# Taking the three lowest weight bits with a ScalarE Copy instead of a VectorE shift, in a fused scan and FFN kernel

## The chip, the core and the metric

The kernel runs on one core of a Trainium2 chip. The metric is the device time of one execution in microseconds, the median of several runs. The engines are TensorE (PE: matmuls, PEld: weight loads), VectorE (DVE), ScalarE (ACT), GpSimd (POOL) and SyncE (SP), whose queue issues nearly all transfers.

## What is computed

A gated linear attention with a complex decay runs over 768 steps for 4 batches and 8 heads of 48 columns; its output is the input of a feed-forward part with a rational activation. The reference, cut to what matters:

```python
for t in range(S):                          # S = 768, D = 48
    S_re, S_im = ar*S_re - ai*S_im + kv, ar*S_im + ai*S_re
    y[:, :, t] = einsum('bhd,bhde->bhe', q[:, :, t], S_re)
x = y.transpose(0, 2, 1, 3).reshape(B*S, H*D)   # 3072 x 384
h = x @ w_in                                     # 384 x 2048
g = (a0 + a1*h + a2*h**2 + a3*h**3) / (1 + |b0|*|h| + |b1|*h**2 + 1e-6)
out = g @ w_out                                  # 2048 x 384
```

`w_in` and `w_out` are 64-bit floats. The kernel gets them as 64-bit words and has to make 32-bit floats of them.

## The kernel before, in words

The sequence is cut into 6 chunks of 128 steps; with 4 batches that makes 24 units, taken in pairs. For a unit `norm` (lines 459 to 487) makes magnitudes and running products, `angle` the phases, `trig` their sines, `outer` the turned q and k, which go through DRAM into the layout HQ, and `attn` (lines 564 to 626) the scores, values and state, and ends in xT, the transposed input of the FFN. `ffn` (from line 629) takes a pair: eight steps k of two 128-row slices of the hidden layer each. The matmuls into ph (line 642) need xT and the weight tiles wi; five ScalarE and four VectorE operations make g out of ph; the matmuls into po (line 659) need g and wo. The first two pairs use the 32-bit weights as they are; then `split` halves each weight into two parts for faster matmuls.

`fold` (lines 407 to 418) makes one 32-bit weight tile of a tile of 64-bit words, 28 times: 12 tiles wi of 128x512 and 16 tiles wo of 128x384. A transfer brings the words into a staging buffer (rings g with four buffers, and wh0, wh1, wh2). An Abs on ScalarE with scale 2^-112 takes the upper word, read as a float, into the tile; a multiplication by zero on VectorE or GpSimd leaves the sign alone in the upper word; a VectorE operation shifts the tile left by 3 and ors the sign in; a second one shifts the lower word right by 29 and ors its three top bits in. Then the staging buffer is free for the next transfer of its ring. These two are in the trace as SCALAR_TENSOR_TENSOR on uint32, with wi or wo as the output.

Nothing is scheduled at run time: every operation is a Plan.op with the engines that it may run on and a cost for each. `recorded` (line 175) reads the order of all 2733 operations, with the engine of each, out of the string ORDER, and they are issued in that order, so each engine and the SP queue run their own part of it in sequence. If an operation waits, all that follows on its engine waits too. ORDER was found by a search over the plan's costs (`list_schedule`).

Of the kernel before, what the change touches and what calls it, by code (L numbers as in the profile page):

```python
# [222 lines left out]


ORDER = (
    "c-lpndwkC2|Ht2-F?L|rHN<As=6o*SPEJLUMF`oxLQRg}oSMj?atb*`q?xlAeJh78Q4ygMDXAf8jyY{cKG$L!#r^(0@B915@8Q8cpZoe;*Zc5#zh19vBH>a|"
    "lH?!#M~zIBdAdhi$v*8UuSr|=q=FRlO)UQgfAS<+Zs{GZDTR7i+UP~CBd0V`3N%bs$|U_=D@p?2#Y%)+(6Z84{?yBQOUp^7Ow-NMTo=h4J;xj8Oon?oQj4wJ"
    "&;>G1OY|OzmBrFkD@i4JUKVLUf7aC!$#;`wnU0XMQdbVEnkjy)jArLNov%Y|Q#Vr2=u|u1UoVepYw0Xicw>$%;QgcezPzDLWPsc&XW9Rf7HcCptrK(tdAv!?"
    "lUY})cgq>=9QAGZ%kGv=;k3D0P5Mfr?DgUU6=az??9UYPG!<NZEs`Gki44^$vPIhIE@{Ayec7dw?d!JaOL9=BYjv3<L&)?a?IUrly;}xJRq3U3r4#SGBl-G<"
    "J|sR-WSUCu3CYsurHL6Y<6OQb$ZdT^zarjVx`IsZlU%JV$zea<sUTCR_*8jZhHFyTkAZ?fr?6djZtCMyVxp|qfm9`$%HIl|pW`jM6Cstndn1pRgh^>2!8;YG"  # L230
    "?3Dy!rMBeBI(<$WnOqkxw|P3=jCGM9psd`Ci7ukV=Bk@vX1Vej<~gmYm*hg=E-zNj2i}&cQeMhwSudUMZ)uFAnu=mwkybZjizX(HIaAMjPM7OHU?E9f(CXe*"
    "9k16llirr-C>^J>WC0Pz%9)tTZmblURqS%Fbkr=#XLlcr_!^}z*$KY&?qZjb(og4^?(TpLHS^s9A}vF0=S!MdqOnE8^>uv<)C}YEM>zu4K9+rfObO@=T}Yj)"
    "%TnpA8S<eX)@JepwI8Do*%U{nbb7XorJk`;XeVErDdUN9jUHsp3XP_ZSrX}`1?I^uDNEd*ZRmQjZ)M&bqtl3Xv23JEs;_~V|C*D2yj<3Lbh^4s)MAtGPm<|c"
    "Uw+q>-V1?-GK7;W$wh4_{lIsBKFflb2_Sr|x#~{?11B{_zZNTlIbp3C;nLZAwLR~z)zjKdv!#sGk`o#ZazE3)62{z316{4837_S~*g<|RdB9}5H`$}5>FHF*"
    "OOYN3WXm9Lpw^QA1n&1%Yd=|SzIQpM&`*>!%>~z4>{(6@$Y9pwnA?75Spo{X66+x?0K297gACAI?IGJuZ?{}iIqgIKXZhxD{me9Rb-{l+{T(V_>o|!sPrJ97"
    "!do#5+$jBzyhDW(v<q1u&~186p3!gUYF~K-7T8F|W5~C^UFw&GYi7tu%{2{OroG$$O&U_q2jy?gGSQOa0vg4+&%y|6wJuYUl+^m{2%;ayB)`w3y<k7{-__TN"
    "<$3vDi@;2=R+X#ztuB{Rv(f*aIvoX#k@RA&US*y?_vdSxybUAW(Cxa?X8HSdfV{4QWRs>4)jrMBAxvFsGI|gkUbIvFoqE~~bgd-b?(*NFzinZhzFNgz@vo7;"
    "m6v6<egO}Tk)|+Sp}eHQC;y^?LnT8;%RBlLOmLFf{}BE;BX<H7y!~d0AIW*1bhFz+Kcz_vJJb)Cmh}96ovnFNUw6wL6X!PTO`WPonBZ1&*_`ux%0~DogG^Ux"
    "dHAIlC@j&*a7{J(n<m|1?H9oESLOp)Y^<*3X&G4$hU(jR_c~o@DGPO(T+vOS{u`L~PrU?lCM7jJTdG%dv<BDiw6px}+JT9#Y&*KHGE7#pW}I#Sk#)&=nXU)X"
    "@7eZ#7dp63&cTnWd(A_x3Y@i8`kL7;MSj*)vRDK&+$Hnv3coy9?Cq+_yV^^ln9gSMoq5U?YG0G-g84L(CPcqkztlBSQ&yPHZk2u`OLZ+BiUNHrwT|gn^t6t)"  # L240
    "E#R+IaIx78ay`r%=TXDuD8P2}g?krXs}0^RlV7s^#Lqy#Qs~ZAeHZK$nsxpdSUFh?Q7xgem%(ytU25977o`tcR-K=Q%Qh6zH?>`fK4Me-A)v4VXGF0gSL4hT"
    "rtJWAeMDZR=FRNipsgI(?E=3vWb%iiI!{S=JxAT{ljlIjO?}a>_k-AY(SGDVBd5XZ3=l9J{JpIg=xT|MrB=g1XE|wX+q(?*iqX^XMO%q-J%~R5+Go@CFF@^C"
    "-KBNxQU3>RV-Ndd*=L^qk$CJ(S9s#ln4zwjSBENO=mmX3lI0WTs4DZAr(NY^Eo(X#MaqBmRid0m9~;R+xtramF?)Hsk<Wg1j=u*apW(DHSszoUC|ldf(~=dF"
    "TC|ajOW}uWX0_X(Tl7gZw<%iP9%c7ns2r2$52H%o!CG15lmp_PwcGuHF!W|Kn10uWqnp}st|j{Zj`_+TZ|k@n<~}eGMpS)p7r!JfK08di!!hsaWg<?;4?Gk4"
    "Zl@kM#-+ji*TKaSyTcFYTpecL^Sj9wB5Th#vsmp>rPHjh!ycYIB)^g89$lnC4qwc)9Ki?7;<FBsHstRlnWc@XM+VQj(ysw>hz>{NiY}RZLCiwdoYCJj)mC>4"
    "^bK|$kDdhGL;$DM!0vJDnWI_oWHue&54QhiexfB_`k6<Vpr7?T8ax=}Jt?o-Hq63NqC8Jco(Z(}c54r_&$eU&zo1_W;oO?MQOM-f$5~~=)YtJkll9*`|Ac)8"
    "$>+K#P}5rvn?5CvNjm%z%sSY!(|Qp8`irb56G@6(F~@bMzl^Fz$?cdvMV(l)RWt1SelC5RO#I_;RhvvpmxaH{G|^0Gj%n`tODeHMlW7(Dy@yE~uTP_Pdttj7"
    "?54US$Y5aPS8XdhKu$ofpa$={5uk21Pflo>UFX-uooo-e$u%%wn)J4t{Rk@e3R<SRKjc1hn6~y*ye0i@gX(tEZFURHn9j2XvRv<y1}O9(dyl_KeqolH@joAS"
    "U7>%W_S1<YfHqYk&S;q+C(Qf2+t?oT%W&Sup(&eS+Q~8h6`d(}h-CzPG6z;z4I^ZN_seijcXB<9gZPrFY+y|Xuv~~{og%tBaKsgS%U0aiBB~10NPB%o-q!QD"
    "=ES7>XZPq<sR4=(>#0Ds*o#`uS7}Y&yKG0llwBSKX^Y^5pG~Z*!P%2=MRP!t^IO6z<vDu?-e{HH#3A;w9sI|c*I()TEc|Q=KQ#sihfE_EAwiGc$#wzvN6lOp"  # L250
    "&x$nW=A?eFgUNplUUHkxH7~hBQw{bircc%2xmW2^w0xHse)b8eM<ng(N<6AntV?v8tTX%lKGMo2`$Kt>OxzXu%%XBbq#aIaCJLKFz7=7-aK713ub(2yEpnU="
    "l<NHwBM-=oP?wWIZmG7AhwV(ivUJjH8|4~H1-r+erJF!~a9*yV%2CoqqHU&&gs+2)*8x}54;4GDpTUB=O_)QyLk!SKK4s!=Fuf^sW2<^zN2Vczn)IYH3ph7V"
    "*VqdFc<OM1JIYb*Zfm>$Rn^xBCVqon(<!o>t}P?8{&?Au=y4&jjKYcBB${lny_FkC3iEXbe|=Jq2gFNde&@17RolTW!b=6H!VMI?FPKl2@sdJKTf^na*K)nX"
    "8pkc=3VV&xi8?m6wVz547lW{T-Dg_3FzGKZnp9j$hSs&M+*a-cGw}SSFy$%TZCCpvm~0ORS%wbvX2KSkU+^5q(D(xFZ$82coCXo!(6>Xp_b4c>4tl$zW4D-)"
    "Qhn0y#o^55ydg|UD)W(Viu{*Q=<Y;19UXcc?R|{*YRLVlK{~E0hm}|8NH$nHq$f>ZDfUmHMGEeI#b4K8-za&`X3)KPbfXze_okKuIWe$TB|5eeROg0fY&N;S"
    "Awf0YVWQY=I^16aZ&i#6WNL~%=I=tKZnF1I{n`#ky9_G6QES@-_b0t*Aw8Ik0=#=7dVN#(qB*0b1N)!C@eRP;W>K-qpb(w+AEHVN><m0$Q)YEGo}#{tg5lb^"
    "`u1KoLEh3srix1l>2^)}@C|Fv={lzUcw&;P;ws7p+y{3~@O2gDIv03TJ^<BU`YE{CgwR}F*GYPv`$s*d_hFf$mO7;Ia}G@QlU}g7{vo{A1NK?B5f?ibh3YBY"
    "^iytvAL$Ox&0!KsaW6TzlS}fN-sbcfx(a8x)c*_o{RL*G+5~@~6qtB74kUf<dz_ue`Ylogb*LyE;lMN64L-fDNnSIY>teXG12ftIcT<_3yh7ahC_xF6G%zXh"
    ">_V9n_zL}-0r&5un;uvRhd~!eGT5q5FJ6;3ZCgLw9)O#YbuYK}fi~aYO{aS^e_7m}hY&-Ml^c-tYNq-CT|7#M+Jq|2?bW>u`xVPn=JN)cb^sUt0e!w?EN<)s"
    "D^J37k=*;My6L)#%GBdV@GAOy8I^2KR-fw+tRE%M()luQ)&y8#uFS{%Hpf>t#l7^TR^@T~*ZGW)(e!U77|aDV*O-K4v_jF?c)D~*>oEJ1c-E1=e1MKTU`M(W"  # L260
    "Xv+fnGZn7MhUKoCRsJM%9;J>3y#?g)DM+u%RNSNGy_wn>b}(pkuxq1W%+a!0gS)pO)}R+!$@Hn>!_dfh-min+rrS;aa-9QTTp-`7(g7Zuz&p2?g^H|xj`_Hx"
    "50Lc$`6qGhnPNJ5ILIM^MqX9<PWtE(ZbvJ)G3+Jk4cxy<$l_yNhRZ(;5B^AeKD_iKHOXV`lX$9F@_9-o%46_uTu85~$x3dJ!O03^kCxQ#G?TZP>Xhmy<_-66"
    "x)vduOo}_Dzvv6pZyaa7XWF7g=^*6<`Zj`mf_JTN?Lts>jrGACkDzvI^hNGw<Cutld1LS(7qyp7_nUD;&15#?h$cZ=+cMl0bG1K;a0+#6rNiKxE!1~UAl%E8"
    "NAbiFyrI<gK`=PSjCQ-Zcg9o0S>|guQft~*9k(r_n5g?;;bK!0N74iA6=+3U%l$-cinTXq-VHjlV7ssUu3(@<12NAQ?VvJCwF10<8Kl;hX7U$G5lw6!&SIwq"
    "eM||RJg5)bIJb+Rdx772tgD3*Tq2TA?7r1>aeL^_K>Bq<5Ar-fwLEarRW5KFxW(<HCu|!5B5K(rSBYKYLN|?{VUdfffnUgND|e)NK?UI!{JS1QwOg?6CVkp#"
    "lHmWV+@a^0J}#)1AEBzz@I^XaBLY9t#a4B}F8+wqC_&SYF{_14{svTOFtJ|Jg><B?l$cuXk_K-iJ7DUXA?K68+*J$ha~h1+b8+xVbm)|9;!hyXOYGQ(S!|Av"
    "3s$BE+Sr8ECA@tC2lz**62Whh<PVs3KNY%2y({CFmCpv~o5ut;m;YDSBPjJfOy4=GU(H=nHHq##Yol0`YudZ(+!Uf<f@`qKpS*pRTeJsC8n7aUn4&@o6AcId"
    "st+?WH#jqoCwp*t`E<UTi{{iDeA^tQ+lnVW2}X8vlPu8SZz=O(caJ^tna)zZZkoD+&>X}ug(Xa38LCo|eWOs3>L~IlZq=7VU8@!P4d?%U(|HH}EiiYvf9QB5"
    "-aSHsH3^s78vN@?S$tzz&I$f0hYtvF##{J=F#ePYJ^eqdrFae"
# [691 lines left out]
```

## Time and profile before

| | |
|---|---|
| median of 3 runs | 622.45 us (619.75 to 622.86) |
| profiled execution | 623.88 us, span 622.17 us |
| mean granted TensorE clock | 0.979 |
| busy share of PE, DVE, ACT, POOL | 88%, 89%, 82%, 49% |
| moved by DMA | 64.87 MB |

How to read it: a busy share is an average over stages. The table of stretches gives busy microseconds of each engine in a stretch of the span; the list of waits tells which engine ended an idle time; the timeline gives single instructions with their start, their duration and, in brackets, the idle time before them and what ended it. A duration includes some overlap with the next instruction of the engine, so the pitch of two neighbours is the better price.

### The profile page before, as it was taken

The numbers are of one execution on the slowest core, as the hardware profiler recorded it, in microseconds if no ns is written. First come the engines' busy times: TensorE is split into PE (matmuls) and PEld (weight loads), VectorE is DVE, ScalarE is ACT, GpSimd is POOL, SyncE is SP. The second block draws the span as 40 slices with busy tenths as digits, with TensorE's granted clock in tenths as the row PEclk, the third lists the DMA queues.
The fourth block names the chain that finished last, engine by engine and source line by source line (L and its number), as shares of the span: only waits on it lengthen the run. The fifth ranks groups of instructions, "written<-read, shape, count | busy, mean of one in ns | idle before, by whom it ended". The sixth has DMA issues, their size and how long they took to land.

```text
...
## 1 busy us (share of the span) xinstructions
PE 546.5 (88%) x6786; PEld 502.1 (81%) x6786; DVE 556.0 (89%) x986; ACT 511.8 (82%) x880; POOL 304.1 (49%) x255
## 2 busy tenths in 40 slices
...
GB/s 307 147 260 252 136 85 157 123 118 134 27 141 98 46 117 105 52 133 72 129 123 75 141 100 54 123 101 147 147 3 106 104 14 143 1 90 2 1 14 44
DMA packets 39109, 64.87 MB, mean 104 GB/s; under 512 B 4464, under 2 KB 26224, under 8 KB 39024
## 3 DMA queue, kind: packets, MB, share of 16 engines
...
q8 instruction: 55, 0.90, 0.7%
q10 hardware_dynamic: 576, 0.52, 0.5%
...
## 4 chain that ended last, share of the span: by engine, by line
PE 51%; DVE 24%; ACT 14%; issue 4%; DMA 4%; POOL 1%; SPq 1%; DVEq 0%; ACTq 0%; POOLq 0%
PE ph L642 21%; PE po L659 20%; DVE A L338 5%; PE bank L609 4%; ACT A L350 4%; PE bank L589 3%; DVE T L338 3%; ACT z L350 3%; DVE z L338 2%; DVE wo L338 2%; DVE wi L338 2%; DVE MM L338 2%; DMA V<-in_v 2%; DVE ST L338 1%; DVE SQ L338 1%
## 5 line engine op out<-in xcount | busy, mean ns | idle before, releaser
L659 PE MATMUL po<-wh,g 128*128 128x384 f32 x640 | 181.1, 340 | 0.8 <-POOL g L338 0.4
L642 PE MATMUL ph<-xT,wiH 128*128 128x256 f32 x960 | 161.4, 286 | 3.3 <-DVE A L338 1.8
L659 PE MATMUL po<-wo,g 128*128 128x384 f32 x428 | 147.2, 383 | 2.2 <-DVE g L338 2.2
L642 PEld LDWEIGHTS ph<-xT,wiH 128*128 128x128 f32 x960 | 135.9, 190 | 6.9 <-ACT xT L350 2.2
L642 PE MATMUL ph<-xT,wi 128*128 128x256 f32 x632 | 127.4, 320 | 8.6 <-DVE wi L338 5.0
L338 POOL TENSOR_TENSOR g<-A,g 128x512 fp32r<-128x512 f32 x52 | 71.4, 1379 | 106.1 <-ACT g L702 60.5
L659 PEld LDWEIGHTS po<-wh,g 128*128 128x128 f32 x640 | 117.2, 188 | 3.2 <-POOL g L338 0.7
L642 PEld LDWEIGHTS ph<-xT,wi 128*128 128x128 f32 x632 | 102.9, 195 | 18.1 <-DVE wi L338 5.4
L659 PEld LDWEIGHTS po<-wo,g 128*128 128x128 f32 x428 | 79.7, 189 | 14.5 <-DVE g L338 3.3
L338 DVE SCALAR_TENSOR_TENSOR A<-A,z 128x512 f32<-128x512 f32 x96 | 65.2, 679 | 25.4 <-ACT z L350 25.3
L350 ACT ACTIVATE z<-A 128x512 f32<-128x512 f32 x96 | 57.5, 599 | 30.3 <-DVE A L338 29.0
L350 ACT ACTIVATE A<-A,co 128x512 f32<-128x512 f32 x96 | 77.9, 812 | 2.9 <-POOL g L338 1.6
L338 DVE SCALAR_TENSOR_TENSOR A<-A,co,ph 128x512 f32<-128x512 f32 x96 | 70.5, 738 | 6.6 <-ACT A L350 6.4
L350 ACT ACTIVATE A<-ph,co 128x512 f32<-128x512 f32 x96 | 65.1, 680 | 6.5 <-DVE A L338 4.5
L338 DVE SCALAR_TENSOR_TENSOR z<-A,z 128x512 f32<-128x512 f32 x96 | 66.3, 691 | 1.8
L350 ACT ACTIVATE A<-ph 128x512 f32<-128x512 f32 x96 | 56.7, 591 | 5.8 <-PE ph L642 5.4
L338 DVE SCALAR_TENSOR_TENSOR A<-A,co,z 128x512 f32<-128x512 f32 x80 | 59.5, 743 | 1.7
L350 ACT ACTIVATE z<-z 128x512 f32<-128x512 f32 x96 | 56.1, 585 | 1.7
L576 PE MATMUL bank<-ident,HQ 96*128 96x96 f32 x160 | 18.0, 249 | 41.8 <-DVE wh L338 37.2
L576 PEld LDWEIGHTS bank<-ident,HQ 96*128 96x128 f32 x160 | 16.3, 142 | 44.9 <-issue 39.9
L338 POOL TENSOR_TENSOR Q<-QK,T 128x768 f32<-128x768 f32 x14 | 29.7, 2120 | 24.5 <-DVE QK L338 13.6
L338 POOL TENSOR_TENSOR QK<-QK,RU 128x768 f32<-128x768 f32 x14 | 29.0, 2074 | 20.7 <-DMA QK<-in_qk 8.1
...
## 6 DMA issues: line engine op xcount, KB each, us to landing
...
```

Source lines behind the costliest of these rows:

```text
L338: call = lambda e: getattr(e, kind)(*map(real, args), **{k: real(x) for k, x in kw.items()})
L350: plan.op(dict(ACT=(act(n, psum) + more, lambda e: e.activation(o(), i(), f, **kw))), r, w)
L576: e.transpose(pt[:, i].bitcast(F32R), hq[0:96, 4 * g + i, 1, :], ident[0:96, 0:96])
L589: e.matmul(pst[m:m + 32, i, 32 * y:C], hf[:, 4 * g + i, 1, 32 * y:32 * y + 32], hf[:, 4 * g + i, 0, 32 * y:C], start=True, stop=True)
L609: e.matmul(py[32 * y:32 * y + 32, min(j, 2), :], l, sts[h // 4][:, h % 4, :] if q is None else hf[:, h, 0, :], start=q is None and j == 0, ...
L642: e.matmul(ph[:, x * T:x * T + T].rearrange("p (h t) -> p h t", h=nb), wt[f // 4 * NJ + j][:, f % 4 * P:f % 4 * P + P], xT[:, x0:x0 + nb, ...
L659: e.matmul(po[b][:, 0:DM], gg[:, b * C:b * C + C], wt[:, 0:DM], start=(f == 0 and n == 0), stop=(f == NFF - 1 and n == len(prods) - 1))
```

## The change

The three lowest bits are no longer ored in by a VectorE operation. After the sign multiplication, which leaves zeros below the sign in the upper word, a ScalarE Copy reads the upper 16 bits of the lower word as an unsigned integer, multiplies by 2^-13, subtracts nearly a half so that rounding gives the floor, and writes the result, 0 to 7, as 16 bits into the lower half of the upper word. The one VectorE operation that is left shifts the tile and ors sign and low bits in together. The plan's cost of a min in `norm` on GpSimd goes up by 630 ns, and ORDER is a new string, searched with these operations and costs. A fold still makes five operations.

```diff
+U16 = mybir.dt.uint16
...
 ORDER = (
...
     def fold(n, src, st):
...
         sign = lambda: high().bitcast(F32)
+        part = lambda y: raw.t.bitcast(U16)[:, :, y]
         scal(AF.Abs, n, f, sign, (raw,), (st,), scale=2.0 ** -112)
         vec("tensor_scalar", n, sign, sign, 0.0, 1.0, ALU.mult, ALU.mult, two=False, r=(raw,), w=(raw,), eng=EN["sign"])
+        scal(AF.Copy, n, lambda: part(2), lambda: part(1), (raw,), (raw,), scale=2.0 ** -13, bias=2.0 ** -14 - 0.5)
         vec("scalar_tensor_tensor", n, i, i, 3, high, ALU.logical_shift_left, ALU.bitwise_or, r=(raw, st), w=(st,))
-        vec("scalar_tensor_tensor", n, i, low, 29, i, ALU.logical_shift_right, ALU.bitwise_or, r=(raw, st), w=(st,))
...
-        vec("tensor_scalar", W, lambda: MM.t, lambda: SQ[:, 1], CLIP2, None, ALU.min, two=False, r=(s1,), w=(MM,), eng=DP)
+        vec("tensor_scalar", W, lambda: MM.t, lambda: SQ[:, 1], CLIP2, None, ALU.min, two=False, more=dict(DVE=0, POOL=630), r=(s1,), w=(MM,),
+            eng=DP)
```

## Rows read from the trace of the kernel before

**Rows 1.** Busy microseconds, share of the span and instructions, from the page.
```profile
PE 546.5 (88%) x6786; PEld 502.1 (81%) x6786; DVE 556.0 (89%) x986; ACT 511.8 (82%) x880; POOL 304.1 (49%) x255
```

**Rows 2.** Stretches: length, busy PE, PEld, DVE, ACT, POOL, clock, DMA share, GB/s.
```profile
0.00:62.00 62.00, 13.81 (x305) 11.98 (x306) 55.53 (x133) 37.14 (x66) 13.47 (x20) 0.90 0.78 241
62.00:130.00 68.00, 57.60 (x479) 42.31 (x480) 64.49 (x128) 61.53 (x103) 29.84 (x33) 0.94 0.43 118
...
130.00:600.00 470.00, 462.03 (x5930) 435.18 (x5929) 427.37 (x707) 407.54 (x703) 258.23 (x201) 1.00 0.38 88
...
80.00:100.00 20.00, 14.99 (x54) 11.19 (x53) 19.08 (x36) 19.74 (x32) 7.77 (x10) 0.91 0.37 128
```

**Rows 3.** Timeline around the first FFN matmul: start, duration, instruction, [idle before <-releaser].
```profile
59.26 0.66 ACT L350 ACTIVATE wi<-wh 128x512 f32<-128x512 f32 x1 [3.22 <-DMA wh<-in_w_in]
...
61.20 0.48 ACT L344 ACTIVATE xT<-bank 128x384 f32<-128x384 f32 x1
...
61.73 10.66 PE L642 MATMUL ph<-xT,wi 128*128 128x256 f32 x36 [3.61 <-ACT xT L344]
```

**Rows 4.** SP queue: one issue (timeline), and waits up to 100 us (total, times, longest).
```profile
51.82 0.33 SPq L332 DMA_DIRECT2D wh<-in_w_in  x1
...
SPq L332 <- DVE wi L338: 19.6, 6, 11.9
```

**Rows 5.** Waits of TensorE up to 130 us: total, times, longest.
```profile
PE ph L642 <- DVE wi L338: 5.0, 1, 5.0
```

**Rows 6.** Timeline of VectorE: its list's first entry, folds, first and last g.
```profile
4.94 0.16 DVE L372 RECIPROCAL co<-ab 128x1 f32<-128x1 f32 x1
...
21.86 0.68 DVE L338 SCALAR_TENSOR_TENSOR wi<-g,wi 128x512 uint32<-128x512 uint32 x1
22.46 0.55 DVE L338 SCALAR_TENSOR_TENSOR wo<-wo,g 128x384 uint32<-128x384 uint32 x1
22.93 0.55 DVE L338 TENSOR_TENSOR SQ<-SQ 128x384 f32<-128x384 f32 x1
...
73.11 0.74 DVE L338 SCALAR_TENSOR_TENSOR g<-A,co,z 128x512 f32<-128x512 f32 x1
...
129.15 0.73 DVE L338 SCALAR_TENSOR_TENSOR g<-A,co,z 128x512 f32<-128x512 f32 x1
```

**Rows 7.** Timeline of ScalarE: Sin, transposes, Abs of folds, squares ahead of g, Copy.
```profile
25.84 0.84 ACT L522 ACTIVATE T<-T 128x768 f32<-128x768 f32 x1 [3.81 <-POOL thc L338]
...
37.91 1.00 ACT L344 ACTIVATE kT<-bank 128x384 f32<-128x384 f32 x2 [5.56 <-PE bank L576]
38.81 0.67 ACT L350 ACTIVATE wi<-wh 128x512 f32<-128x512 f32 x1
39.38 0.55 ACT L350 ACTIVATE wo<-wh 128x384 f32<-128x384 f32 x1
39.84 0.56 ACT L350 ACTIVATE wo<-g 128x384 f32<-128x384 f32 x1
...
69.72 0.59 ACT L350 ACTIVATE z<-z 128x512 f32<-128x512 f32 x1
...
123.78 0.83 ACT L522 ACTIVATE T<-T 128x768 f32<-128x768 f32 x1
...
124.88 0.62 ACT L350 ACTIVATE wiH<-wi 128x512 fp32r<-128x512 f32 x1
125.40 0.58 ACT L350 ACTIVATE z<-z 128x512 f32<-128x512 f32 x1
```

**Rows 8.** Groups up to 160 us, by shape: count, busy us, mean ns, idle before.
```profile
L350 ACT ACTIVATE A<-A,co 128x512 f32<-128x512 f32 x14 | 11.3, 808 | 0.2
...
L350 ACT ACTIVATE wiH<-wi 128x512 fp32r<-128x512 f32 x12 | 7.3, 617 | 0.1
...
L350 ACT ACTIVATE wi<-g 128x512 f32<-128x512 f32 x6 | 4.0, 665 | 1.9 <-DMA g<-in_w_in 1.9
```

**Rows 9.** The chain that ended last: start, duration, what.
```profile
19.95 5.87 POOL thc L338
```

More of the change, by code (lines that the diff above doesn't have):

```diff
@@ L225 @@
 ORDER = (
[L226 to L269, printed above, removed]
+    "c-k$P34G7>AIIO{Nw#6151VUYGiUCzoE14jA&a@YT*)2H5YjR#b4Ds8azvA>!<pqssVEX=*5MlU{cP;;|MPqQpTGG(Jo@do@4ny9_w#<gj`!<RS-GiAB~?ah"
@@ new lines @@
+    "l>Aq3Xt-38T^cE#<f{4qe~l$ebBaC#dP}Rzzgks(;k%U+(ofIo`+R;WFYB8!K+8x#Z)&VK)(GdWNL$v;=5J9vwN_r!KXi#Sm(F_2#JEYaQcr3*nIY@-j3&!6"
+    "KC8;BlBPo>QLl678#+TmMA_98y%N?af0TrAZL-vpN&14ktD|jQH%3orL&?)jT`dcAqHNa*@`%0_Qa&(MH&MqBoh3^&J|r$sMKW}jJ|Lr{m_*CpTAbRGbv?Ut"
+    "I#Wupi$v+IZ_5gevV&YLeOX4xWE1ITNP)IDE!}3hs>?Ntx~s@U`N>;)cOCbal^>;zzALHJm!SXXJN7T%lbQOHoY0BvXQsYE1yy94whn0$h|vY|v@B+ivv}ts"
+    "lj1_;EzLC6jh9;Tm3O%GDtAsVtFcM`KFN(3?JjE=J$3q?e5k+aB3Y|LSmUbhkUiQ<zSC)1+>6wyQcZ@_gQId<Q@J}#K9NpRTMO910$s_~TY(g>vYwMgI$jo-"
@@ new lines @@
+    "1V7HZt(EmJttBs0&6nC=l68{!fp9ONWmUX<eVaQg%LIK_2TC#>yP<aj0jZ@)VEL8|qf;foI6p80bf(76%?gouFz8d6Z~C~Lfc5SdjgXu>I>~(K5<%f+Al3fp"
+    "AJrRjHSnfg<Vw-k7<pb_XPqG?P5*VH>HJ(*QcHT*b&3wt750X|TBhoY`k*&aXTquNauB8zlgSz)Df}!(e_zsS-s!+ck`z|5;7XvHH(eXaaZL;hE10dzWTolk"
+    "=BWqE%E@YT%ukl{fwfXnrbrnn)KzpqO<gw@c9)R3x>0`R=f~PZLS?f#<0nd4?j5W3q^W)^4@zH9xW;}uc?0wg>?|Xd?QH)yy-ha?HAUCJw`uYLJm_OSbtB3|"
+    "`=OGgsovtiAa8lZFn02chRR`iNtS9Z{Vgk2CYV=Uk}4~_hdu&Y%m(~w@Us-U9160Z=nOmDuOg$V`VD$EPpjI#t}*Kllm;@??9%65iXG@rk^Z2xLFa3VWa}Vl"
@@ new lines @@
+    "u1)lW)X}fKSeQMS%1-JPeOkWI4)9?|pr_Z=ZuP550&Bjj6{WXqgL%azQyw$<esA<xL0Z~1?j7wNC{cE`UqBaEXrkt@LY!%svqVSApL*JKbNAER%en$(o-#Gu"
+    "Qkb1ARrG@S)g{Kv$@)m6P4S#meMY9sn{>B?d=s-LYl@DrtNhQjCmg$_dvq}hS!h@L${i=QuDq|-KI=XN%T(Ld?~7_%>2!Hs;`CYhRR5!&+v2Xb_LaGES8LOW"
+    "Rl#R$2mckk;C-q;jK?f>{d52h5-PXp;dOtIc9gBAtBZl_L*%G_As@lm1LiSQn5JD}^M3xi2o`RT(f&E^372>oqZ-pSYl#jApO^52W+u_Krw1d^(sHdW&&UvI"
+    "B?EOCTG}JkP}|S?r9LI&QFfwz$BzWT4blt+Y|!&M2F|YJ-CHyj#m?8$xI?Z!VR!%giHxO|dUAo4QgOiHHr9{u#(>D{`hlF&G}&hwx?$Q(e%C^NdylT|mTl&7"
@@ new lines @@
+    "7q4}_%)tFP_+lBSt!x8VNq5o3r)9Iodd)%ohz_<rU4f?Q=XAWcynye%BTG#k_c;C8rwL$i8~m1N2CPpIUuU54KO-vSB-%^=KETcz$RXXPEo3iMSCDV1dn_(?"
+    "TKmW;R{zob<)`ts?x4F1kIb;0{X*TqE<^Fbs@(UG>_D^6aL*od$=@&edK!&a^md}BQ)ZI?HQpY9D$?cC()+vyu7<QXpRnUls+!C!xMr%mY_rMl4%b4YG@aU~"
+    "*G*4%P`k0#HdNjhr)Yydli0x$@LX>yy4Lco=?tPtaC|ZT(H_Ny^KXtWm3n5kE7ZO8BL!Wp)z)aFzElLofoQp-wCAZVwi6zZ0_WD@@7X$mYaPrJE|I$Gqp0Dm"
+    "dr}Y3&DMHbdg$Lc&mOHN8Rj)P>i5BKSK-E;m_xtd3)`qUpiQI&b%x<9{bN^NOp=9K-yZjK!EO!;8$<<RvNU3ulQJFM65Q^p-ls`kMdoT-D$mFDGtC9R4Qteq"
```

27 lines of the change are left out of this document (added).

## The prediction

> **What bounds the kernel now.** I read the page's busy times first: TensorE, VectorE and ScalarE all lie between 82% and 89% of the span [rows 1], so no single engine explains 622 us. The table of stretches splits it [rows 2]. From 130 to 600 us TensorE is busy 462.03 of 470: it is the bound there, and VectorE (427.37) keeps up. Before that TensorE is not: it works 13.81 of the first 62 us, and from 62 to 130 it still lacks 68 - 57.60 = 10.4 us. In the same stretches VectorE is busy 55.53 of 62 and 64.49 of 68, ScalarE 37.14 and 61.53. So the kernel is a fill of about 120 us set by VectorE, with ScalarE loosely loaded up to 62 us and tight after it (19.74 of 20 from 80 to 100), and then a stretch of TensorE's. What shortens the fill shortens the span, as long as TensorE is not starved later.
>
> Three edges of the fill are to be seen. The first FFN matmul starts at 61.73, after 3.61 us of waiting for ScalarE's copy of xT at 61.20; that copy stands in ScalarE's queue behind an Abs of a weight load, which waited 3.22 us for a transfer [rows 3] that was issued at 51.82, when its staging buffer came free [rows 4]. The longest wait of TensorE after that is 5.0 us, for a wi tile from VectorE [rows 5]. And SP, which issues in order, spent 19.6 us in six waits for VectorE's wi results, up to 11.9 us at once: it waits for staging buffers to be emptied [rows 4].
>
> **The new order.** recorded() turns both ORDER strings into lists of 2733 operations, each with its engine; the length is the same, since fold() still makes five. I place the two lists beside the trace of before and add up pitches (start to start of neighbours that don't wait, the median of each kind); no op's duration is taken from anywhere else. In before the VectorE list up to the last g of the first FFN call is 213 entries, from 4.94 us to 129.15 (first and last of [rows 6]), 115.8 us of pitches. ScalarE's list up to the square that feeds this g (start 125.40 [rows 7]) is 87.1; reloads of activation tables behind a Sin pass are left out on both sides.
>
> **Part 1, the operation removed from VectorE.** Each of 28 folds loses its shift-and-or. Its pitch is 0.60 us for 512 columns and 0.47 for 384 (22.46 - 21.86, 22.93 - 22.46 [rows 6]): 12 x 0.60 + 16 x 0.47 = 14.7 us. All 28 lie ahead of the last g of the first FFN call, in the stretch VectorE bounds, so all count. The new list gives 3.5 back ahead of this place: four more sign multiplications on VectorE instead of GpSimd (+1.2), one more angle scan (+1.7), small exchanges for the rest. 115.8 - 14.7 + 3.5 = 104.6. Up to the first g: 63.9 before (done at 73.85 [rows 6]), 56.3 after.
>
> **Part 2, the Copy added to ScalarE.** The trace has no 16-bit write on ScalarE, so the price is bounded. The nearest row is the Abs of the same fold, which reads the same words at the same 8-byte step: 0.57 us pitch at 512 and 0.46 at 384 (39.38 - 38.81, 39.84 - 39.38 [rows 7]). From below stands the contiguous Copy of halve (mean 617 ns against 665 of the Abs), from above the slowest activation of 512 columns (808 ns) [rows 8]. I take the Abs, with its medians: 12 x 0.58 + 16 x 0.45 = 14.2; bounds 14.2 x 617/665 = 13 and 14.2 x 808/665 = 17. I charge no table load: in before a Copy (124.88) follows the pass of Sin and Arctan (123.78) without one [rows 7]. ScalarE's list up to the square of the last g goes from 87.1 to 99.5 (other moves take 1.8 off); up to the first one from 39.1 (start 69.72 [rows 7]) to 51.9. ScalarE had that room up to 62 us (62 - 37.14 = 25 us idle), not after it.
>
> The Trainium skill (ScalarE: Activation LUTs, section Rules for kernel authors) tells one to use VectorE and not ScalarE for adds and multiplies, with VectorE up to about three times as fast per element in bf16. This trace does not agree for this pair: the two-operand VectorE op takes 0.60 us and a ScalarE pass over the same words 0.57. By the rule ScalarE would lose more than VectorE wins, and the sum would be about zero; that is the second rival below.
>
> **Part 3, the chain of a fold.** Abs, sign, or, or becomes Abs, sign, Copy, or: VectorE's second hop becomes a hop to ScalarE and back. The new wait is ScalarE's for the sign result, and behind it in ScalarE's queue stand the Abs of the next folds, xT and the FFN's activations. The new list hides it by distance: between a fold's Abs and its Copy stand 2 to 11 other ScalarE ops in the first part of the list. The staging buffer now comes free after one VectorE op of the fold instead of two; the list frees the first g buffer behind 12.3 us of VectorE work where it was 17.0.
>
> **Part 4, when the first g comes.** *VectorE's way.* It begins about 6.2 us into the span (an estimate) instead of 4.94, since its first entry is now a norm op that needs a transfer and a Square. T is complete after 11.7 us of work, near 18.4. GpSimd's copy of thc, the first op of its list before and after, took 5.87 us [rows 9] and held the Sin pass for 3.81 [rows 7]; it stays, so the Sin results are there near 25.8 and VectorE, with 16.4 us of work ahead of them, waits 3 us. The ST ops of the first unit need HQ transfers that leave only after that; I estimate 3 more us. With 1 to 2 for the rest: 56.3 + 6.2 + 3 + 3 + 1.5 = 70. *ScalarE's way.* It is held until 25.8 with 18.1 done, then for TensorE's first transposes until near 37.4 (37.91 in before [rows 7]) with 25.6 done, then, by my estimate, until near 46 for the first xT with 33.0 done; 51.9 - 33.0 = 18.9 more, 1 to 2 for transfers and 2 for the VectorE ops that follow: 68.5. The later is 70: 4 us sooner than 73.85. The first FFN matmul should move from 61.7 to about 57: the gating transfer follows the release of its buffer at about 47 instead of 51.8.
>
> **Part 5, from there to TensorE's own stretch.** Before, 115.8 - 63.9 = 51.9 us of VectorE work took 129.9 - 73.9 = 56.0. Now it is 104.6 - 56.3 = 48.3; with the same 4.1 of waiting, 52.4, 3.6 sooner. ScalarE has 47.6 where it had 48.0 and took 55.7 (69.72 to 125.40), so it does not decide. Sum: 4 + 3.6 = 7.6 us, inside what TensorE lacks (4.7 at its first FFN matmul and up to 10.4 in the stretch to 130).
>
> **Part 6, the rest.** The plan's cost of min on GpSimd rises by 630 ns, and yet the new list puts 19 of 24 there (15 in before); fewer multiplications of outer() go there. With all engine choices and the shuffled tail VectorE gets 4.8 us more after the last g of the first FFN call, in a stretch where it has 470 - 427 = 43 idle. TensorE hides that mostly; I charge 0.2. The end (last matmul, eviction, stores) has the same ops.
>
> Total -7.4. The profiled execution took 623.88 with a span of 622.17; the median of the runs is 622.45, and the shift applies to that: **615.0 us**.
>
> **Rivals.**
> - *ScalarE takes VectorE's place.* For: 19.74 of 20 busy from 80 to 100, and both lists are now near 100 us at the last g (104.6 and 99.5), so each waits for the other more often. If the waiting of part 5 doubles and part 4 yields 2, the gain is 2: 620.5. Against: in before the two ran at 91% and 87% of 470 us together and TensorE lost only 8.
> - *Slower: the Copy is dearer than the Abs* (a 2-byte write at an 8-byte step, or the rule above). ScalarE's last square would come near 118 against 125.4, so 28 Copies decide from 7.4/28 = 0.26 us extra each; at 0.6 extra, about double, 17 us more on ScalarE: 632 at worst, 626 with half of it hidden. Against: the strided Abs row.
> - *TensorE starves later.* The new list leaves VectorE 2 us ahead instead of 12 at some places of the middle (g of the fourth chunk), and adds 4.8 us: 3 to 5 us lost, 619.
> - *More than forecast.* SP's 19.6 us of waits go, transfers come early, the first matmul starts at 52 and the 5.0 us wait for wi vanishes: 609.
>
> **How the numbers follow.** Forecast 0.50 (611 to 619), more than forecast 0.13, starving later 0.13, ScalarE as the bound 0.14, slower 0.10. A measurement of this kernel tells about 0.5% (3.1 us) from no change. Faster: 0.50 + 0.13 + half of 0.13 = 0.70; slower 0.10; same 0.20. The range 607 to 623 leaves out the slower case and the tail of the large gain.
>
> **What would show it.** Right: VectorE's fold ops fall by 28, ScalarE gets 28 activations of at most 0.7 us, the first FFN matmul starts at 55 to 59, the last g of the first FFN call ends at 119 to 125 instead of 129.9, TensorE's idle time between 62 and 130 falls below 8, and its stretch after that stays at 98%. Wrong: Copies over 0.9 us; ScalarE waiting for GpSimd's or VectorE's sign results ahead of xT; an unchanged first matmul; or a TensorE that idles more than 10 us between 130 and 600.

## The result and the profile after

The changed kernel takes 617.76 us (median of 13 runs, 615.99 to 620.53), the kernel before in the same comparison 622.86: a ratio of 0.9918, 95% interval [0.9893, 0.9943], about 5.1 us faster. Below, a ratio becomes microseconds by multiplying its distance from 1 by 622.9. The profiled execution of after took 616.93 us with a span of 615.2, 7.0 us under that of before, so the two profiles lie 1.9 us further apart than the medians. Behind the diff's added lines, L338, L344, L350, L522, L642 and L659 of before are L339, L345, L351, L525, L645 and L662.

The page's line of busy times (as in [rows 1]): ScalarE is up by 25.8 us, VectorE down by only 6.7, TensorE the same.

```profile
PE 546.7 (89%) x6786; PEld 502.2 (82%) x6786; DVE 549.3 (89%) x968; ACT 537.6 (87%) x907; POOL 281.4 (46%) x247
```

The stretches of [rows 2] in after (length, busy PE, PEld, DVE, ACT, POOL, clock, DMA share, GB/s); the third ends 7 us earlier, as the span does:

```profile
0.00:62.00 62.00, 17.21 (x312) 14.92 (x313) 51.06 (x114) 58.87 (x90) 7.88 (x23) 0.88 0.87 260
62.00:130.00 68.00, 60.72 (x493) 44.16 (x492) 62.35 (x129) 66.93 (x109) 31.06 (x29) 0.96 0.50 121
130.00:593.00 463.00, 456.00 (x5907) 430.77 (x5906) 425.90 (x703) 405.34 (x699) 241.16 (x195) 1.00 0.37 86
```

The gain lies in the fill: TensorE has done 17.21 + 60.72 = 77.9 us of work by 130 us, where before it had done 71.4. After that it idles 7.0 us, before 8.0. But the engine that is full in the fill is another one. ScalarE, at 37.14 of 62 before, is now busy 58.87 of 62 and 66.93 of 68, and VectorE is the engine with gaps.

The reason stands in the groups of the Copy and of the fold's Abs up to 160 us (count, busy us, mean ns of one, idle before):

```profile
L351 ACT ACTIVATE wh<-wh 128x384 uint16<-128x384 uint16 x8 | 8.6, 1069 | 0.0
L351 ACT ACTIVATE g<-g 128x384 uint16<-128x384 uint16 x8 | 8.5, 1068 | 0.0
L351 ACT ACTIVATE wh<-wh 128x512 uint16<-128x512 uint16 x6 | 8.2, 1370 | 0.0
L351 ACT ACTIVATE g<-g 128x512 uint16<-128x512 uint16 x6 | 8.1, 1344 | 0.7 <-DVE g L339 0.7
...
L351 ACT ACTIVATE wo<-wh 128x384 f32<-128x384 f32 x8 | 4.5, 560 | 0.0
L351 ACT ACTIVATE wi<-wh 128x512 f32<-128x512 f32 x6 | 4.1, 685 | 0.0
```

A Copy takes twice as long as the Abs over the same words: 33.4 us busy in all. The timeline of ScalarE ahead of the first FFN matmul gives the pitch and the damage (start, duration, instruction):

```profile
51.77 1.36 ACT L351 ACTIVATE g<-g 128x512 uint16<-128x512 uint16 x1
52.85 0.70 ACT L351 ACTIVATE wiH<-wi 128x512 fp32r<-128x512 f32 x1
...
54.00 1.09 ACT L351 ACTIVATE g<-g 128x384 uint16<-128x384 uint16 x1
54.81 0.72 ACT L351 ACTIVATE wi<-wh 128x512 f32<-128x512 f32 x1
55.43 2.20 ACT L351 ACTIVATE wh<-wh 128x384 uint16<-128x384 uint16 x2
...
57.97 0.48 ACT L345 ACTIVATE xT<-bank 128x384 f32<-128x384 f32 x1
```

512 columns have a pitch of 52.85 - 51.77 = 1.08 us, 384 of 54.81 - 54.00 = 0.81: 12 x 1.08 + 16 x 0.81 = 25.9 us of ScalarE's time. Four Copies stand in the six microseconds before xT, and TensorE waits for xT:

```profile
58.50 13.79 PE L645 MATMUL ph<-xT,wi 128*128 128x256 f32 x48 [2.64 <-ACT xT L345]
```

It starts 3.2 us sooner than in [rows 3]. The first and the last g of the first FFN call on VectorE, and GpSimd's thc copy (the last phases of a chunk, kept for the next), to be set against [rows 6] and [rows 9]:

```profile
72.27 0.74 DVE L339 SCALAR_TENSOR_TENSOR g<-A,co,z 128x512 f32<-128x512 f32 x1
...
126.17 0.75 DVE L339 SCALAR_TENSOR_TENSOR g<-A,co,z 128x512 f32<-128x512 f32 x1
```

```profile
19.00 0.50 POOL L339 COPY thc<-T 128x6 f32<-128x6 f32 x1 [14.62 <-DVE T L339]
```

The first g ends at 73.01 (73.85 before), the last at 126.92 (129.88). VectorE's list got lighter and ScalarE's heavier, and SP's waits for wi results went from 19.6 us [rows 4] to 16.0.

### The profile page after: what moved, and what is told of

The parts are those of the page before. It is cut to its first block, busy times and chain, and to the rows that moved or that the text cites. A ratio compares the mean times of both kernels' runs of the same rounds, so it can differ in the third digit from the quotient of the medians.

```text
span 615.2 us, 16716 instructions
## 1 busy us (share of the span) xinstructions
PE 546.7 (89%) x6786; PEld 502.2 (82%) x6786; DVE 549.3 (89%) x968; ACT 537.6 (87%) x907; POOL 281.4 (46%) x247
## 4 chain that ended last, share of the span: by engine, by line
PE 42%; DVE 19%; ACT 18%; DMA 8%; issue 6%; POOL 5%; SPq 1%; POOLq 0%; DVEq 0%; ACTq 0%
PE po L662 18%; PE ph L645 16%; DVE A L339 5%; PE bank L612 4%; DMA HQ<-Q 3%; ACT g L351 2%; PE bank L592 2%; ACT A L351 2%; DVE z L339 2%; DMA AA<-in_aa 2%; ACT z L351 2%; ACT SQ L351 2%; ACT wh L351 2%; DVE MM L339 1%; DVE ST L339 1%
## 5 line engine op out<-in xcount | busy, mean ns | idle before, releaser
L662 PE MATMUL po<-wh,g 128*128 128x384 f32 x640 | 180.9, 339 | 0.0
L645 PE MATMUL ph<-xT,wiH 128*128 128x256 f32 x960 | 161.7, 287 | 2.3 <-DVE A L339 1.7
L662 PE MATMUL po<-wo,g 128*128 128x384 f32 x428 | 146.5, 383 | 0.8 <-DVE g L339 0.8
L645 PEld LDWEIGHTS ph<-xT,wiH 128*128 128x128 f32 x960 | 136.0, 190 | 5.6 <-ACT z L351 2.0
L645 PE MATMUL ph<-xT,wi 128*128 128x256 f32 x632 | 128.3, 322 | 7.5 <-DVE A L339 3.9
L339 POOL TENSOR_TENSOR g<-A,g 128x512 fp32r<-128x512 f32 x48 | 65.7, 1377 | 115.5 <-ACT g L705 63.2
L662 PEld LDWEIGHTS po<-wh,g 128*128 128x128 f32 x640 | 117.3, 188 | 1.0 <-issue 0.2
L645 PEld LDWEIGHTS ph<-xT,wi 128*128 128x128 f32 x632 | 102.6, 195 | 17.0 <-DVE A L339 5.4
L662 PEld LDWEIGHTS po<-wo,g 128*128 128x128 f32 x428 | 79.8, 189 | 13.6 <-DVE g L339 1.5
L339 DVE SCALAR_TENSOR_TENSOR A<-A,z 128x512 f32<-128x512 f32 x96 | 65.2, 679 | 23.8 <-ACT z L351 23.4
L351 ACT ACTIVATE A<-A,co 128x512 f32<-128x512 f32 x96 | 77.9, 812 | 3.7 <-DVE g L339 1.8
L351 ACT ACTIVATE z<-A 128x512 f32<-128x512 f32 x96 | 57.9, 603 | 26.4 <-DVE A L339 24.4
L339 DVE SCALAR_TENSOR_TENSOR A<-A,co,ph 128x512 f32<-128x512 f32 x96 | 70.8, 739 | 4.0 <-ACT A L351 4.0
L339 DVE SCALAR_TENSOR_TENSOR z<-A,z 128x512 f32<-128x512 f32 x96 | 66.3, 691 | 1.8
L351 ACT ACTIVATE A<-ph 128x512 f32<-128x512 f32 x96 | 56.9, 593 | 11.2 <-PE ph L645 9.3
L351 ACT ACTIVATE A<-ph,co 128x512 f32<-128x512 f32 x96 | 65.2, 680 | 0.3
L339 DVE SCALAR_TENSOR_TENSOR A<-A,co,z 128x512 f32<-128x512 f32 x80 | 59.4, 743 | 1.4
L351 ACT ACTIVATE z<-z 128x512 f32<-128x512 f32 x96 | 56.5, 589 | 1.5
L592 PEld LDWEIGHTS bank<-HQ 96*32 96x32 f32 x1536 | 31.1, 114 | 10.4 <-ACT kT L345 6.1
L592 PE MATMUL bank<-HQ 96*32 96x128 f32 (+3 forms) x1536 | 34.7, 244 | 4.3 <-ACT kT L345 3.9
```

The costliest lines, as they stand in the source:

```text
L339: call = lambda e: getattr(e, kind)(*map(real, args), **{k: real(x) for k, x in kw.items()})
L592: e.matmul(pst[m:m + 32, i, 32 * y:C], hf[:, 4 * g + i, 1, 32 * y:32 * y + 32], hf[:, 4 * g + i, 0, 32 * y:C], start=True, stop=True)
L645: e.matmul(ph[:, x * T:x * T + T].rearrange("p (h t) -> p h t", h=nb), wt[f // 4 * NJ + j][:, f % 4 * P:f % 4 * P + P], xT[:, x0:x0 + nb, ...
L662: e.matmul(po[b][:, 0:DM], gg[:, b * C:b * C + C], wt[:, 0:DM], start=(f == 0 and n == 0), stop=(f == NFF - 1 and n == len(prods) - 1))
```

## Experiments

**What makes the Copy dear.** Written behind the end of the kernel after, single operations of 512 columns run three times each; in the trace they stand among its last operations:

```diff
+        H4 = lambda y: W8.bitcast(U16)[:, :, y]      # 16-bit part y of 8-byte words
+        F2 = lambda y: W8.bitcast(F32)[:, :, y]      # 32-bit half y of the same words
...
+        act_(H4(2), H4(1), AF.Copy, **kw)             # L931, the fold's Copy
+        act_(cu_, H4(1), AF.Copy, **kw)               # L933, contiguous result
...
+        act_(H4(2), cf_, AF.Copy, **kw)               # L941, f32 source
...
+        act_(F2(0), cf_, AF.Copy)                     # L945, f32 result at the step
+        act_(cb_, cf_, AF.Copy)                       # L947, bf16 result, contiguous
+        act_(sb_[:, :, 0], cf_, AF.Copy)              # L949, bf16 result at the step
...
+        nc.vector.tensor_scalar(H4(2), H4(1), 13, None, ALU.logical_shift_right)    # L953
+        nc.gpsimd.tensor_scalar(H4(2), H4(1), 2.0 ** -13, 2.0 ** -14 - 0.5, ALU.mult, ALU.add)  # L955
```

> The changed kernel with a measuring part behind its end: groups of three ScalarE passes over 512 columns, each with one trait of the fold's Copy, then three of the same on VectorE and on GpSimd. In the profile of the changed kernel the Copy took 1.34 to 1.37 us at 512 columns, where 0.67 was forecast. Theory W (16-bit write at a step of 8 bytes): every pass that writes 16 bits with a step takes 1.3 us, whatever it reads, and the contiguous ones 0.6. Theory C (conversion to an integer): the contiguous uint16 write is as slow, 1.3 us, and the bf16 write at the same step is not, 0.6. Theory R (16-bit read at a step): the pass from the same words to contiguous float is slow, 1.3 us. Theory N (reading and writing the same 8-byte words): only the in-place passes are slow, the 32-bit one too. On VectorE I expect the one-source shift at 0.4 us, on GpSimd 0.7.

Groups of this part (the run took 636.07 us with it):

```profile
L931 ACT ACTIVATE w<-w 128x512 uint16<-128x512 uint16 x3 | 4.1, 1378 | 0.0
...
L955 POOL TENSOR_SCALAR w<-w 128x512 uint16<-128x512 uint16 x3 | 4.0, 1322 | 17.8 <-DVE w L953 17.6
L941 ACT ACTIVATE w<-cf__8136 128x512 uint16<-128x512 f32 x3 | 4.0, 1321 | 0.0
L949 ACT ACTIVATE sb__8140<-cf__8136 128x512 bf16<-128x512 f32 x3 | 4.0, 1320 | 0.0
...
L953 DVE TENSOR_SCALAR w<-w 128x512 uint16<-128x512 uint16 x3 | 2.2, 736 | 0.7 <-ACT w L945 0.7
L945 ACT ACTIVATE w<-cf__8136 128x512 f32<-128x512 f32 x3 | 2.1, 706 | 0.0
L933 ACT ACTIVATE cu__8137<-w 128x512 uint16<-128x512 uint16 x3 | 2.0, 662 | 0.0
...
L947 ACT ACTIVATE cb__8139<-cf__8136 128x512 bf16<-128x512 f32 x3 | 1.9, 630 | 0.0
```

Of the traits tried only the write matters. A 16-bit result at an 8-byte step costs 1.32 to 1.38 us from each source tried and in either 16-bit type; a 32-bit result at the same step costs 0.71, and the same 16-bit read with a contiguous result 0.66. Other steps were not tried. On VectorE it is also dear: 0.74 against 0.42 for the 32-bit sign operation, also one-source, at this step, here in the trace of before:

```profile
23.87 0.42 DVE L338 TENSOR_SCALAR g<-g 128x512 f32<-128x512 f32 x1
```

**The fold alone, the order alone.** First the new fold in the order of before, then the new order with the old fold:

```diff
 # fold alone: fold() of after, but
-ORDER = (... of after)
+ORDER = (... of before)
 # order alone: after with
-        scal(AF.Copy, n, lambda: part(2), lambda: part(1), (raw,), (raw,), ...)
-        vec("scalar_tensor_tensor", n, i, i, 3, high, ...)
+        vec("scalar_tensor_tensor", n, i, i, 3, high, ...)
+        vec("scalar_tensor_tensor", n, i, low, 29, i, ...)
```

> The new fold with the order of before: the Copy stands where the first or stood, the one or where the second stood. Theory F (the removed VectorE operation carries the gain): 616 to 619, as the changed kernel. Theory O (the new order carries it, and the dear Copies need the room that it makes on ScalarE): ScalarE's list up to the last square of the first FFN call grows from 87 to 120 us in the 125 that it has, so 624 to 630, slower than before. The first FFN matmul stands at 62 or later in O, at 58 in F.

> The new order with the fold of before: the first or stands where the Copy stood, on VectorE. Theory F: VectorE's list up to the last g of the first FFN call is 119 us, more than the 116 of before, and so 622 to 626. Theory O: the order has gains of its own (GpSimd's copy of thc at 0.5 us instead of 5.9), 617 to 620. If both parts are needed together it is above both, and the sum of the two single effects misses the joint one.

The fold alone is slower, 1.0121 [1.008, 1.0162], +7.5 us; its median of 632.90 lies above even the 624 to 630 of the theory that the order carries the gain. The order alone changes nothing that can be told, 0.9979 [0.9952, 1.0006]; its 623.19 lies in the range of the theory that the removed operation carries it. Together they give 0.9918, so neither part earns the gain by itself. The stretches of the fold alone, and of the order alone:

```profile
0.00:62.00 62.00, 14.08 (x304) 12.25 (x304) 47.21 (x115) 50.98 (x79) 5.65 (x20) 1.00 0.75 231
62.00:130.00 68.00, 47.43 (x359) 33.91 (x363) 51.21 (x100) 63.40 (x102) 23.39 (x27) 0.90 0.43 119
```

```profile
0.00:62.00 62.00, 15.12 (x310) 13.38 (x311) 57.32 (x127) 38.78 (x67) 13.33 (x23) 1.00 0.83 252
62.00:130.00 68.00, 57.10 (x477) 42.10 (x476) 65.69 (x136) 57.17 (x96) 26.93 (x24) 0.92 0.46 114
```

In the fold alone both engines idle (47.21 and 50.98 of 62; VectorE 51.21 of 68). It is VectorE that waits for ScalarE: up to 130 us its waits for ScalarE add up to 22.3 us, ScalarE's for VectorE to 3.6. The largest of each (total, times, longest):

```profile
DVE A L339 <- ACT z L351: 6.0, 4, 3.1
...
ACT SQ L351 <- DVE MM L339: 2.0, 2, 1.7
```

In the order alone VectorE is as full as before. GpSimd's thc copy did not take the 0.5 us that the theory of the order counted on but 5.06 there, and the Sin pass waited for it:

```profile
25.18 0.84 ACT L524 ACTIVATE T<-T 128x768 f32<-128x768 f32 x1 [3.00 <-POOL thc L339]
```

What the order gives without this wait was not run.

**The change at the forecast price.** After, with Copies that move 32-bit words (it leaves out the three lowest bits of the weights):

```diff
-        scal(AF.Copy, n, lambda: part(2), lambda: part(1), (raw,), (raw,), scale=2.0 ** -13, bias=2.0 ** -14 - 0.5)
+        scal(AF.Copy, n, lambda: low().bitcast(F32), sign, (raw,), (raw,), scale=2.0 ** -13, bias=2.0 ** -14 - 0.5)
```

> The changed kernel with the Copy reading and writing 32-bit words at the same step (from the upper word into the lower); it leaves out the three lowest bits of the weights. If the 16-bit form is what makes the Copy dear, the 28 Copies fall from 33 us to 15 us. Theory S (ScalarE bounds the fill of the changed kernel because of the dear Copies): 611 to 614, 4 to 6 us faster than the changed kernel. Rival V (VectorE or the transfers bound the fill, the dear Copies are hidden): within 1.5 us of 617.8.

```profile
L351 ACT ACTIVATE wh<-wh 128x384 f32<-128x384 f32 x8 | 4.5, 563 | 0.7 <-POOL wh L339 0.7
L351 ACT ACTIVATE wh<-wh 128x512 f32<-128x512 f32 x6 | 4.0, 668 | 0.0
```

The Copies cost what the forecast assumed, and the ratio is 0.9814 [0.9773, 0.9855], -11.6 us: the dear write takes 6.5 us from the change, of the 11.7 that it adds to ScalarE's time. TensorE's first FFN matmul, and the first and last g:

```profile
54.72 8.07 PE L645 MATMUL ph<-xT,wi 128*128 128x256 f32 x36 [0.81 <-ACT xT L345]
```

```profile
67.20 0.74 DVE L339 SCALAR_TENSOR_TENSOR g<-A,co,z 128x512 f32<-128x512 f32 x1
...
119.21 0.75 DVE L339 SCALAR_TENSOR_TENSOR g<-A,co,z 128x512 f32<-128x512 f32 x1
```

The last g ends at 119.96, 7.0 us before that of after; this is where the 6.5 us are.

**No Copy at all.** This, too, leaves out the three lowest bits:

```diff
-        scal(AF.Copy, n, lambda: part(2), lambda: part(1), (raw,), (raw,), ...)
+        plan.op(dict(ACT=(act(n), lambda e: None)), (raw,), (raw,))
```

> The kernel after without any Copy; it leaves out the three lowest bits of the weights. It says what the whole Copy costs and what is the bound without it. If VectorE is the bound as soon as the Copy is at the price that was forecast, it is as fast as the run with 32-bit Copies within 2 us: 610 to 614. If each Copy on ScalarE, cheap or dear, costs time, another 14 us of ScalarE's work go and it takes 603 to 608.

0.9792 [0.9725, 0.9859]. The median of 609.29 lies between the two ranges named, nearer to that of the theory that VectorE bounds it then. Taking the other 14 us of Copies off ScalarE as well gives 1.4 us more by the ratios and 3.0 by the medians (612.28 and 609.29), inside the intervals: from the forecast's price upward 6.5 of 11.7 us count, from there downward at most a small part of 14 that this run can't tell from nothing.

**The low bits on the other engines.** After's order, with another engine at the Copy's place:

```diff
-        scal(AF.Copy, n, lambda: part(2), lambda: part(1), (raw,), (raw,), scale=2.0 ** -13, bias=2.0 ** -14 - 0.5)
 # GpSimd
+        vec("tensor_scalar", n, lambda: part(2), lambda: part(1), 2.0 ** -13, 2.0 ** -14 - 0.5, ALU.mult, ALU.add, two=False, ..., eng=("POOL",))
 # VectorE
+        vec("tensor_scalar", n, lambda: part(2), lambda: part(1), 13, None, ALU.logical_shift_right, two=False, ...)
```

> The kernel after, its order kept, but GpSimd makes the low bits, by a multiplication and an addition on the same 16-bit parts, at 1.0 to 1.4 us each, some 33 us in the first 130, where it is busy 39 of them. ScalarE loses 25.6 us and VectorE nothing. If GpSimd's operations run while VectorE is busy, the fill is VectorE's and the kernel takes 608 to 613. If GpSimd is held off by VectorE's work, as the 6-element copy at the start of the kernel before seemed to be (5.87 us), its fold operations are spread out to 2 us and more, the folds come late, and it takes 622 to 635.

> The kernel after, its order kept, with the low bits made by VectorE: a 16-bit shift of one source at the Copy's place, 0.74 us for 512 columns when measured alone. ScalarE loses 25.6 us, VectorE gets 28 operations of 0.50 to 0.68, about 16. If what the change wins is that VectorE is relieved, this gives it all back: 622 to 627, no better than before. If what it wins is mostly the new order and the earlier release of the staging buffers, 616 to 619.

On VectorE: 0.9956 [0.9926, 0.9986], between the two theories: by the ratios about half of the gain goes back, and the interval overlaps that of after. On GpSimd: 1.0043 [1.0008, 1.0078], in the range of the theory that VectorE holds it off. Two of its groups, and the first operation of the upper one:

```profile
L339 POOL TENSOR_SCALAR wh<-wh 128x512 uint16<-128x512 uint16 x6 | 13.1, 2185 | 4.8 <-DVE wh L339 4.6
...
L339 DVE SCALAR_TENSOR_TENSOR wi<-wi,wh 128x512 uint32<-128x512 uint32 x6 | 5.9, 978 | 3.6 <-POOL wh L339 3.6
```

```profile
16.61 4.95 POOL L339 TENSOR_SCALAR wh<-wh 128x512 uint16<-128x512 uint16 x1 [3.29 <-DVE wh L339]
```

```profile
19.82 0.55 DVE L339 SCALAR_TENSOR_TENSOR RU<-Z,RU 128x384 f32<-128x384 f32 x1
21.59 0.69 DVE L339 SCALAR_TENSOR_TENSOR wi<-wi,wh 128x512 uint32<-128x512 uint32 x1 [1.22 <-POOL wh L339]
```

What takes 1.32 us alone took 4.95 while VectorE ran without a gap. It ended at 21.56, 1.19 us after VectorE's operation of 19.82 was done (20.37), and VectorE, which waited for it, went on at 21.59. The delay goes the other way too: VectorE got no operation more than in after, but its busy time is 563.2 us against 549.3, and its fold operation of the rows above took 0.98 us in the mean where it took 0.69 in after. So the loss is not all GpSimd's waiting.

**Trading between the two engines.** Three ways to take load off ScalarE at VectorE's cost. In the first, 9 of 28 folds keep the old two VectorE operations. In the second the Copy writes 32 bits, and the sign operation is a masked or of two words. In the third only the 20 folds whose sign VectorE makes have that form:

```diff
 # first
+        if len(loads) % 3 == 0:
+            vec("scalar_tensor_tensor", n, i, i, 3, high, ...)
+            vec("scalar_tensor_tensor", n, i, low, 29, i, ...)
+            return
 # second; third: for the folds other than 6, 12, 15, 17, 19, 22, 24, 27
-        vec("tensor_scalar", n, sign, sign, 0.0, 1.0, ALU.mult, ALU.mult, ..., eng=EN["sign"])
-        scal(AF.Copy, n, lambda: part(2), lambda: part(1), ...)
+        scal(AF.Copy, n, low, lambda: part(1), ...)
+        vec("scalar_tensor_tensor", n, high, high, 2 ** 31, low, ALU.bitwise_and, ALU.bitwise_or, r=(raw,), w=(raw,))
```

> The kernel after, its order kept, but 9 of the 28 folds (every third) take the low bits with the old VectorE shift-and-or in place of ScalarE's Copy. ScalarE loses 9 Copies of 0.80 to 1.07 us, about 8.2 us; VectorE gets 9 operations of 0.47 to 0.60 us, about 4.7. If ScalarE alone now sets the fill, the gain over the kernel after is near half of that difference and more, 3 to 5 us: 613 to 615. If VectorE's work is worth as much as ScalarE's there (the two wait for each other), the gain is at most 1: 617 to 619. If what helped was that every fold frees its staging buffer after one VectorE operation, it is slower than after: 620 or more.

> The kernel after, but the Copy writes its result as a 32-bit integer over the lower word, and VectorE's operation for the sign is one that masks the sign bit and ors the low word in; the result is the same. No 16-bit write is left. If the 16-bit write at an 8-byte step is what makes the Copy dear, the Copies take 0.55 to 0.70 us, ScalarE loses 11 to 12 us; VectorE pays 0.15 us more for each of 20 sign operations and 0.5 for the 8 that GpSimd had, 7 us. With ScalarE as the only bound of the fill this gives back most of the 5.5 us that cheap Copies alone gave: 612 to 614. With VectorE just behind it as the next bound, 615 to 618.

> The kernel after with both forms: 20 folds, those whose sign is made on VectorE, use the Copy with a 32-bit result and the masked or; the 8 whose sign is made on GpSimd keep the Copy with the 16-bit result. ScalarE loses 20 x 0.4 = 8 us, VectorE gets 20 x 0.15 = 3. If ScalarE alone sets the fill of the kernel after, 3 to 5 us are won: 613 to 615. If the two engines wait for each other so that work taken from one counts only as far as none is put on the other, 1 to 2: 616 to 617.

The first gives 0.992 [0.9885, 0.9954], the second 0.9906 [0.987, 0.9942], both not to be told from after: the theory of two engines that wait for each other. The third gives 0.9857 [0.9816, 0.9898], 3.8 us under after, nearer to the theory that ScalarE alone counts. In the second the Copies fall to the Abs's price, as the bench said:

```profile
L351 ACT ACTIVATE g<-g 128x384 uint32<-128x384 uint16 x8 | 4.2, 540 | 0.0
...
L351 ACT ACTIVATE g<-g 128x512 uint32<-128x512 uint16 x6 | 4.0, 658 | 0.0
```

The trade in numbers, as busy microseconds of the whole execution against after's page:

| against after | ScalarE | VectorE | time |
|---|---|---|---|
| 32-bit Copies | -13.1 | -0.1 | -6.5 |
| third form | -9.0 | +6.3 | -3.8 |
| 32-bit result in all folds | -12.7 | +8.5 | -0.7 |
| 9 old folds | -8.2 | +8.1 | +0.1 |
| low bits on VectorE | -25.7 | +13.4 | +2.4 |
| order alone | -25.2 | +15.2 | +3.8 |

Each time is a difference of two ratios and uncertain by some 3 us, so single rows don't weigh much. In the last two rows ScalarE is relieved of 10 to 12 us more than VectorE is charged, and the time does not fall: a microsecond put on VectorE seems to cost at least what one taken off ScalarE saves. The third form, which buys 9 for 6, is the only one of the trades with VectorE that gains more than 1 us.

The rows differ in one thing more, the thc copy at the start. It took 0.51 us in the third form, but 5.06 with the 9 old folds, and there the Sin pass waited for it (total, times, longest), as in the order alone:

```profile
ACT T L529 <- POOL thc L339: 3.0, 1, 3.0
```

By the next experiment such a wait is worth some 3 us, so it can be the whole difference between the first and the third form, and it weakens what the rows say of the two engines' loads. No run separates the two.

**One copy moved.** The first thc copy, of 6 elements, from GpSimd to VectorE, in the kernel before and in the third form:

```diff
-            vec("tensor_copy", 2 * NJ, th, lambda: last(C - 1), r=(T,), w=(key,), eng=EN["carry"])
+            vec("tensor_copy", 2 * NJ, th, lambda: last(C - 1), r=(T,), w=(key,), eng=EN["carry"] if c or bb else ("DVE",))
```

> The kernel before with one operation moved: the first 6-element copy of thc, 5.87 us on GpSimd, runs on VectorE. If GpSimd was held off by VectorE's uninterrupted work, the copy takes 0.1 to 0.3 us there and the Sin pass no longer waits 3.81 us. If that wait was a cause of the late first unit, as the forecast for the changed kernel assumed when it charged 3 us for it, the kernel gains 2 to 4 us: 620.5 to 622.5 where before is at 624.5. If the fill of the kernel before is VectorE's list anyway, ScalarE's wait is covered and it stays within 1 us of before.

> The kernel of both forms, and the first thc copy on VectorE. Where VectorE has a gap while GpSimd copies, as in the kernel after (0.50 us), nothing is to be won. Where it has none, the copy takes 3 to 5 us on GpSimd and the Sin pass waits 1 to 3; then this wins up to 2 us over the kernel of both forms: 611 to 615. If the wait is covered, the two are within 1 us.

In the kernel before: 0.9949 [0.9918, 0.998], -3.2 us (1.2 to 5.1) for one operation of 0.16 us. The copy, and the Sin pass that had waited 3.81 us for it until 25.84 [rows 7]:

```profile
19.99 0.16 DVE L338 COPY thc<-T 128x6 f32<-128x6 f32 x1
```

```profile
22.00 0.84 ACT L522 ACTIVATE T<-T 128x768 f32<-128x768 f32 x1
```

In the third form the copy had taken only 0.51 us on GpSimd; moving it gives 0.9842 [0.9799, 0.9885], 614.67 us. That is not told apart from the third form, but its interval lies below that of after: this version beats both kernels.

## Why the prediction was right, and where its steps were not

The forecast was 615.0, and 617.76 came out: the direction and the size hold, but as the sum of two errors of opposite sign, and that they nearly cancel is luck. With the Copies at the forecast price the change gives -11.6 us, not -7.4; the dear write then takes 6.5 back.

- *Part 1* held: 28 operations left VectorE. Its busy time fell by 6.7 us in all; the steps gave -14.7 + 3.5 + 4.8 = -6.4, with the work that the new order puts there.
- *Part 2* failed. The Copy was priced as the Abs, 14.2 us with 17 as the upper bound; it measured 25.9. The bounds came from rows with 32-bit writes, and the range didn't reach past them. The step went wrong by choosing the nearest row by what is read (the same words, the same step), while the price hung on what is written. The forecast named a 2-byte write at this step as a rival, with Copies over 0.9 us as its sign, and they took 1.07 to 1.37 in the means of their groups.
- *That rival's time was wrong too.* It let the extra decide from 0.26 us each and came to 626 to 632. The extra is (25.9 - 14.2)/28 = 0.42 us, and the kernel is still faster than before. The rival took ScalarE's slack as 7.4 us; but ScalarE had 25 us idle before 62 [rows 2], which the new order used up, and the gain without the extra is 11.6.
- *Part 3* held for the wait that it names: that for the sign result is small (0.7 us ahead of the Copies in the groups above). It left out VectorE's wait for the Copy, the hop back. Up to 130 us the VectorE operation that is left in a fold waited 4.4 us for Copies in after, more than half of it here (total, times, longest):

```profile
DVE wi L339 <- ACT wh L351: 2.3, 2, 1.7
```

- *Part 4* had two wrong terms. The thc copy did not stay at 5.87 us; it took 0.50, and the Sin pass began at 23.65, 2.2 us sooner than in [rows 7], held by ScalarE's own list now. And ScalarE's way, given as 68.5, has 22 Copies before the square that feeds the first g, 9 us more at the measured pitches; 5.1 of them show (73.01 against 67.94 with cheap Copies), and the first g came 0.8 us sooner, not 4. The first matmul, at 58.50, lies inside the 55 to 59 named. With cheap Copies it is at 54.72, and the first g ends at 67.94 where 70 was forecast: the waits put on VectorE's way were too long by 2 us.
- *Part 5* is right at its own price: from the first to the last g 52.0 us with cheap Copies (119.96 - 67.94), 52.4 forecast. With the real ones it is 53.9, and the sentence that ScalarE does not decide there is wrong: it is busy 66.93 of 68. So the last g ends at 126.92, outside the 119 to 125 named.
- *Part 6* held: TensorE idles 7.3 us between 62 and 130, below the 8 named, and runs at 456.00 of 463 after that. Starving later did not come.
- *ScalarE takes VectorE's place* happened, at 617.8 instead of 620.5.

The Trainium skill's rule (ScalarE: Activation LUTs, Rules for kernel authors) to do adds and multiplies on VectorE looked wrong by the Abs row. For the low bits as they are taken, the rows agree with it: 0.74 us for VectorE's shift against 1.38 for ScalarE's Copy. For this kernel the engine's load weighs as much: with the bits on VectorE the ratio is 0.9956, no better than the 0.9918 on ScalarE. The forecast gave two times for this rule, a sum of about zero and the second rival's 626 to 632; 617.76 is neither. The same page (section Step-by-step: what each stage is for) gives one time per element for fp32 and bf16 alike; the bench does not agree where the bf16 result has an 8-byte step, 1.32 us against 0.63 contiguous.
